# Tile 25's last rounding steps into slots 0 and 1 of block 1, tile 26 into slots 1 and 2, and batch 2's products of q one slot on

## The chip, the core and the metric

The kernel runs on one core of a Trainium2 chip. The metric is device time of one execution in microseconds (us): the median of five runs. The engines are TensorE (PE in the profile), VectorE (DVE), ScalarE (ACT), GpSimd (POOL) and SyncE (SP), which here only issues transfers. Each works through its own queue in order, and semaphores hold an instruction until what it needs is there.

## The reference

Two layers follow each other, all in float32:

```python
# q, k, v: (8 batches, 8 heads, 576, 64); g_norm: (64,)
kv  = einsum('bhsd,bhse->bhde', k, v)
out = einsum('bhsd,bhde->bhse', q, kv)
out = out / sqrt(mean(out * out, -1) + 1e-6) * g_norm
x   = out.transpose(0, 2, 1, 3).reshape(4608, 512)
h   = x @ w_in                       # w_in (512, 2048)
y   = maximum(0.01 * h, h) @ w_out   # w_out (2048, 512)
```

The weights come in as float64 and are rounded to float32 on the chip.

## The kernel before

**Blocks and units.** The 4608 rows of x are cut into 9 blocks of 512. A block goes through the two weight products in chunks of d_ff, 512 columns each (four chunks, numbered 0 to 3). Block 0 begins with plain products over chunks 0 to 2, in `first_block`; then comes block 1 over all four chunks, then chunk 3 of block 0, then blocks 2 to 8. One block and chunk is a *unit*. In a unit each of the two products is done in Strassen's manner with seven products, in the order 1, 2, 6, 5, 7, 3, 4.

**Slots.** The main loop gives each of the seven products h of a unit one *slot*: block 1 has slots 0 to 27, chunk 3 of block 0 has slots 28 to 34. A slot issues one product h (eight matmuls, 1.73 us from start to start), and from slot 9 on also one product o of an earlier unit, which stand in `o_queue` and lag by two slots. In slots 0 to 8 there is no product o beside the products h. The results of products h lie in four PSUM banks, `ha`, `hc`, `hb`, `hd`. Product 6 is added in the same bank on top of product 1, so it waits until ScalarE has copied product 1 out (L938); product 5 starts the second bank afresh, so it waits until VectorE has added product 2 into g (L698). In the same way product 7 waits for the copy of product 6 (L945), product 3 for the copy of product 5 (L940), and product 4 for VectorE's sum of product 7.

**Rounding the weights.** A weight tile (32 of them, `w_jobs`) is rounded by the generator `round_f64`, seven steps long: two ScalarE casts (L264 `add`, L262 `cut`), VectorE's clamp (L266), an empty step, the *sign* step on ScalarE (L271), VectorE's shift-and-or (L281) and, as the last step, VectorE's 16-bit add (L284). Tiles up to 25 are started in `first_block` by `round_w`, which does the first three steps and leaves the rest to `finish_w`; a table `plan` says at which half step which tile starts (a number) and where the open one is finished (`f`). From tile 26 on the main loop does the steps, 3, 3 and 1 in three slots, by the queue `rest`. Tiles 24 to 27 are the four tiles of w_out for chunk 3; chunk 3 is not used before slot 21.

**GpSimd and the writes.** GpSimd forms the sums of weight tiles and of g that the Strassen products take (`sides_w1`, `sides_w2`, `combine`, `sums_of`). Many are written to DRAM for the later blocks; SyncE issues these writes (L735) in a fixed order, behind the four writes of block 0's part sums `o` (`part<-o`), which VectorE (L1158) and ScalarE (L1156) copy out of PSUM at the end of `first_block`. The buffer `pairs` is used again as soon as its write has landed.

**Attention beside it.** `attention(b)` is a generator too: it turns q (L505), forms kv = k'v in PSUM, copies it to SBUF (`copy_kv`, L371), then for each block that the batch touches issues the products of q with kv (`outputs`, step for e = 0 and step for e = 1) with squares and scaled copies on ScalarE (L415, L421), sums of squares (L419), transposes and reductions (L430, L431), the root (L436), the reciprocal (L440), its spreading (L444), a transpose back and the multiply of x (L450, L452). The table `A_SLOTS` says how many steps of batch 2's attention are taken in which slot. Batch 2's first part writes 384 rows of block 2.

```python
            for t in range(7):
                slot = 7 * c + t
                go(h_steps, 1)
                ...
                    if rest:
                        go(steps, rest.popleft())
                    ...
                    go(a_steps, A_SLOTS.get(at, 0))
```

Of the kernel before, what the change touches and what calls it, by code (L numbers as in the profile page):

```python
# [24 lines left out]
def kernel(  # L25
# [121 lines left out]
    def load_some(n=1):  # L147

        while to_load and n > 0:
            b, p, what = to_load.popleft()  # L150
            load_pair(b, p, what)
            n -= 1
# [157 lines left out]
    def rounding(j, high_first=False):  # L310
        if w_in.dtype == I64:
            yield from round_f64(w_jobs[j][0], w_raws.pop(j), high_first)

    halfway = collections.deque()
# [15 lines left out]
    def finish_w():  # L330
        while halfway:
            for _ in halfway.popleft():
                pass
# [597 lines left out]
    def product_h(n, w_sides, x_sides, to):  # L931

        g11, g21, g22, g12 = g_of(n)

        def done(i, bank):

            if i == 1:
                first_turn(nc.scalar.copy(g11, bank))  # L938
            elif i == 5:
                first_turn(nc.scalar.copy(g22, bank))  # L940
            elif i == 2:
                add(nc.vector, g11, bank, g11, pinned=True)
                relu(g11)
            elif i == 6:
                first_turn(nc.scalar.copy(g21, bank))  # L945
            elif i == 3:
                add(nc.vector, g21, bank, g21, pinned=True)
                relu(g21)
            elif i == 7:
                add(nc.vector, g22, bank, g22, pinned=True)  # L950
                relu(g22)
            else:
                relu(g12, bank)

        yield from strassen((("ha", "hc"), ("hb", "hd"))[n % 2], lambda i, part, r: w_sides[i][:, part, r, :],
                            lambda i, part, r: x_sides[i][:, r, :], done)
        sums_of(n, to)
# [142 lines left out]
    def go(steps, n=None):  # L1100
        while n is None or n > 0:
            if next(steps, steps) is steps:
                return
            n = None if n is None else n - 1
# [20 lines left out]
    def first_block(between):  # L1125
# [27 lines left out]
        for t in range(4):  # L1153
# [9 lines left out]
    t, a, f, x = "tafx"  # L1163
# [2 lines left out]
            (5, 0): (13, f, a), (5, 1): (14, f), (6, 0): (15, f), (6, 1): (16, f),  # L1166
            (7, 0): (a, a, 17, f), (7, 1): (a, 18, f), (8, 0): (19, f, a, 20, f),
            (8, 1): (21, f, a), (9, 0): (a, a, a, a, a, a, 22, f), (9, 1): (x, 23),
            (10, 0): (f, 24), (11, 0): (f, 25), (12, 1): (f,)}
    loaded, x_sides = 12, None  # L1170

    def between(n, half):
        nonlocal loaded, x_sides
        for what in plan.get((n, half), ()):
# [7 lines left out]
            else:  # L1182
# [9 lines left out]
    first_block(between)  # L1192
    in_first = False
    first_done = True
    rounded, rest = 26, collections.deque()
    in_block_1 = True
    pin(nc.gpsimd.tensor_copy(pair(0, NW)[:1, :1], x_sides[4][:1, 0, :1]))
    h_sides, more = sides_w1(0)
# [4 lines left out]
    in_loop = True  # L1203

    LATE_ONE = {15: 2, 16: 2, 17: 1, 18: 1, 19: 2}
    A_SLOTS = {18: 1, 19: 2, 22: 1, 23: 1, 24: 2, 25: 1, 26: 1, 27: 2, 28: 1, 29: 1, 30: 1, 31: 1,
               34: 2}
    DIRECT = {25: ((1, (0, 1)), (3, (1,))), 27: ((2, (0, 1)),), 29: ((3, (0,)),)}
    READS = {26: 2, 28: 4, 30: RING}
    PARTS = {33: ("11", "12"), 35: ("22",), 37: ("21",)}  # L1210
# [13 lines left out]
    def second_of(n):  # L1224
        if n in seconds:
            os_, finish = seconds.pop(n)
            return Second(n, os_["11"], finish)
# [9 lines left out]
    for i, chunks in rounds:  # L1237
        one = in_block_1 = i < 2
        steady = not one
        if i == 1:  # L1240
            late, a_steps = a_steps, attention(2)
        elif i > 1:
            late, a_steps = a_steps, attention(i + 1, fine=True) if i + 1 < B else iter(())
        os = {}
        for c in chunks:
            now += 1
            nxt = units[now + 1] if now + 1 < len(units) else (NB, 0)
            g_sides = {}
            h_steps = product_h(now, h_sides, x_sides, g_sides) if one else \
                product_h_two(i, c, now, quarters, g_sides, second_of(now - 2))  # L1250
# [3 lines that stand above are left out]
                if not one:  # L1254

                    if t == 6:
                        go(h_steps, 1)
                    if slot in LATE_SLOTS:
                        go(late, 1)
                    for _ in range(FINE_SLOTS.get(slot, 0)):  # L1260
                        go(a_steps, 1)
                    if i + 1 < NB:
                        if slot == 20:
                            x_sides, new_quarters, sums, inner = sides_x(i + 1)
                        if slot in (20, 21, 22):
                            go(sums, 2 if slot == 20 else 1)
                        if slot == 24:
                            inner(0)
                        elif slot == 25:
                            inner(1)  # L1270
                    load_some()

                if now - 1 in seconds:
                    for half in range(2):
                        if t == (6 if half else 4):
                            inner_g(now - 1, half)
                    if t == 5 and now - 1 < 2 * NC + NC - K:
                        inner_w2(units[now - 1][1])
                if (7 * now + t == 7 * NC + 4):
                    while writes:  # L1280
                        pin(nc.sync.dma_start(*writes.pop()))
                if slot in HELD and i == NB - 1:
                    pass
                elif waited == LAG:
                    go_o()
                elif o_queue:
                    waited += 1
                write_later()
                at = 7 * now + t
                for key in PARTS.get(at, ()):  # L1290
                    if at == 33:
                        part_os = os
                    load_part(part_os, key)
                if at in READS:
                    read(READS[at])
                if one:
                    if not rest and rounded < len(w_jobs):
                        steps = rounding(rounded)
                        rest.extend((3, 3, 1))
                        rounded += 1  # L1300
                    if rest:
                        go(steps, rest.popleft())
                    if loaded < min(rounded + 2, len(w_jobs)):
                        load_w(loaded)
                        loaded += 1
                    for chunk, only in DIRECT.get(at, ()):
                        go(combine(chunk, 2, only=only))
                    if at == 18:
                        direct_0 = combine(0, 2, nc.vector)
                    if at in (18, 19, 22, 23):  # L1310
                        go(direct_0, 1)
                    if t == 3 and nxt[0] < 2 and nxt[1] != c:
                        h_sides, more_h = sides_w1(nxt[1])
                        if now == 0:
                            go(combine(0, 1))
                    if t == 5 and nxt[0] < 2 and nxt[1] != c:
                        more_h()
                    if t == 0 and units[now - 1][1] != c and now > 0:
                        for part in range(2):
                            go(combine(c, part))  # L1320
                    if at in (15, 16):
                        load_pair(2, at - 15)
                    go(late, LATE_ONE.get(at, 0))
                    go(a_steps, A_SLOTS.get(at, 0))
                    load_some(2 if at in (19, 20, 24, 25) else 1)
                    if at == 7 * NC - 4:
                        x_sides, _, sums, _ = sides_x(0)
                    elif at == 7 * N1 - 4:
                        x_sides, new_quarters, sums, inner = sides_x(2)
                    if at in (7 * NC - 4, 7 * NC - 3, 7 * N1 - 4, 7 * N1 - 3):  # L1330
                        go(sums, 2)
                    if at == 7 * N1 - 3:
                        inner(0)
                    elif at == 7 * N1 - 2:
                        inner(1)

            for _ in range(2 if i == NB - 1 and c == NC - 1 else 0):
                go(h_steps, 1)
                go_o()
            go(h_steps)  # L1340
            if c == NC - 1 and i != 1 and i + 1 < NB:
                inner(2)
                quarters = new_quarters
            by_two = NC + NC - K <= now < len(units) - 2
            if by_two:
                seconds[now] = (os, store(i))
            o_queue.append(product_o(now, g_sides, os, store(i), by_two))
# [32 lines left out]
```

## Time and profile before

| | |
|---|---|
| median of 5 runs | 919.46 us (919.02 to 920.09) |
| the profiled execution | 920.02 us, its span 918.3 us |
| PE busy | 907.2 us (99%) |
| DVE, ACT, POOL busy | 623.2, 347.6, 392.1 us (68%, 38%, 43%) |
| granted TensorE clock | 1.000 |

The span is the time from the first to the last instruction of the profiled execution; 1.7 us of its time lie around it. Times in the timeline count from the start of the span. A busy PE is no PE at its peak, as matmuls are pipelined and their ends are modelled; the start-to-start times are the safer reading. A wait for several semaphores is put down to the one that came last by the profile, and where the engine named had long been done it was another. Block 1 begins at about 113 us and ends at about 205 us, chunk 3 of block 0 ends at about 230 us.

### The profile page before, as it was taken

To read this page: it belongs to the slowest core of one execution; us is meant where nothing else is said; L and a number is where in the kernel's file an instruction comes from. 1 tells how busy PE (TensorE), PEld (TensorE's weight loads), DVE (VectorE), ACT (ScalarE), POOL (GpSimd) and SP (SyncE) were. 2 spreads that over 40 slices of the span, in tenths; PEclk is the share of its full clock that TensorE was granted. 3 is DMA by queue.
4 is the path that set the end of the run, shared out by engine and by line. 5 is a ranking of instruction groups with operands and counts; after the bars stand their busy time and mean duration, and the time that the engine had idled before them with its cause. 6 is when DMAs were issued, how large, how long until landed. Compare 5 with 4: busy or idle time off the path is not lost.

```text
span 918.3 us, 18136 instructions
## 1 busy us (share of the span) xinstructions
PE 907.2 (99%) x7024; PEld 783.9 (85%) x7024; DVE 623.2 (68%) x1127; ACT 347.6 (38%) x679; POOL 392.1 (43%) x467
## 2 busy tenths in 40 slices
PE   8999989999999999999999999999999999999998
PEld 4444478878998999899999999999999999999997
DVE  5765865767656876687756876678669755755565
ACT  5756454221335233433243334332443333223330
POOL 2000479959733473226421642264226522542222
PEclk9999999999999999999999999999999999999999
DMA  8998175896999678867886789757765676567632
GB/s 256 217 251 233 57 222 181 261 301 199 348 329 290 213 223 263 232 231 218 250 258 217 233 245 264 229 168 221 237 180 174 194 218 201 182 190 220 201 108 92
DMA packets 92405, 202.16 MB, mean 220 GB/s; under 512 B 10016, under 2 KB 44448, under 8 KB 92320
## 3 DMA queue, kind: packets, MB, share of 16 engines
q1 hardware_dynamic: 81344, 189.14, 68.6%
q10 hardware_dynamic: 10528, 10.69, 3.4%
q8 instruction: 56, 0.92, 0.4%
q0 software_dynamic: 448, 1.18, 0.3%
q14 instruction: 29, 0.24, 0.1%
HBM read 173.44 MB, written 27.53 MB: 219 GB/s over the span
## 4 chain that ended last, share of the span: by engine, by line
PE 77%; DMA 8%; POOL 7%; DVE 4%; issue 2%; ACT 1%; SPq 0%; POOLq 0%; ACTq 0%; DVEq 0%
PE o_c L126 17%; PE o_a L126 17%; PE h_ha L126 11%; PE h_hb L126 11%; PE h_hc L126 8%; PE h_hd L126 8%; POOL pairs L698 3%; PE o_ps L126 3%; POOL stage L698 2%; DMA stage<-in_moe_w_in_dram 2%; POOL gs L698 2%; DMA v_in<-in_v_dram 1%; DMA q_in<-in_q_dram 1%; DMA pairs<-in_moe_w_out_dram 1%; DMA pairs<-in_v_dram 1%
## 5 line engine op out<-in xcount | busy, mean ns | idle before, releaser
L698 POOL TENSOR_TENSOR gs<-g 128x512 f32<-128x512 f32 x66 | 84.1, 1274 | 249.0 <-ACT g L913 249.0
L913 ACT ACTIVATE g<-g 128x512 f32<-128x512 f32 x127 | 80.2, 631 | 148.6 <-DVE g L698 148.5
L1032 ACT COPY w_all<-h_ha 128x512 f32<-128x512 f32 x84 | 49.0, 583 | 169.7 <-PE h_ha L126 159.6
L126 PE MATMUL o_c<-pairs,gs 128*128 128x256 f32 x392 | 93.2, 381 | 0.0
L126 PE MATMUL o_a<-pairs,gs 128*128 128x256 f32 x392 | 93.0, 380 | 0.0
L698 DVE TENSOR_TENSOR o<-h_hb,o 128x128 f32<-128x128 f32 x104 | 29.9, 287 | 83.5 <-ACT pairs L1032 83.4
L126 PEld LDWEIGHTS o_c<-pairs,gs 128*128 128x128 f32 x392 | 71.3, 190 | 9.4 <-POOL pairs L698 1.2
L126 PEld LDWEIGHTS o_a<-pairs,gs 128*128 128x128 f32 x392 | 71.3, 190 | 8.1
L698 DVE TENSOR_TENSOR o<-o_a,o 128x512 f32<-128x512 f32 (+1 forms) x93 | 62.6, 673 | 22.0 <-PE o_a L126 21.7
L698 DVE TENSOR_TENSOR o<-o_c,o 128x512 f32<-128x512 f32 x80 | 54.7, 684 | 26.2 <-PE o_c L126 26.0
L126 PE MATMUL h_ha<-stage,w_all 128*128 128x128 f32 x448 | 59.6, 276 | 0.0
L126 PEld LDWEIGHTS h_ha<-stage,w_all 128*128 128x128 f32 x448 | 56.6, 192 | 3.0 <-issue 0.7
L698 DVE TENSOR_TENSOR g<-g,pairs 128x512 f32<-128x512 f32 x84 | 55.7, 689 | 1.9
L698 POOL TENSOR_TENSOR pairs<-g 128x128 f32<-128x128 f32 x52 | 23.8, 457 | 76.1 <-PE h_hb L126 47.4
L698 DVE TENSOR_TENSOR w_all<-h_hc,w_all 128x512 f32<-128x512 f32 x56 | 38.3, 685 | 15.7 <-PE h_hc L126 15.3
L698 DVE TENSOR_TENSOR o<-h_hd,o 128x128 f32<-128x128 f32 x78 | 22.2, 284 | 38.1 <-ACT pairs L1032 38.0
L126 PE MATMUL h_hb<-stage,w_all 128*128 128x128 f32 x336 | 46.7, 275 | 0.0
L698 POOL TENSOR_TENSOR gs<-g,gs 128x512 f32<-128x512 f32 x33 | 46.2, 1400 | 0.0
L698 POOL TENSOR_TENSOR gs<-gs,g 128x512 f32<-128x512 f32 x33 | 45.0, 1364 | 2.6
L1032 ACT COPY pairs<-h_hb 128x384 f32<-128x384 f32 x84 | 40.1, 477 | 13.2 <-PE h_hb L126 12.6
L126 PE MATMUL o_acc<-w,g 128*128 128x512 f32 x96 | 43.7, 598 | 0.6 <-DVE w L284 0.3
L126 PE MATMUL h_ha<-xT,w_all 128*128 128x128 f32 x224 | 43.3, 275 | 0.1
(240 smaller groups left out, 2245.1 us busy)
## 6 DMA issues: line engine op xcount, KB each, us to landing
w_all<-w SPq DMA_DIRECT2D x196, 448.0 KB, 4.1
pairs<-w SPq DMA_DIRECT2D x56, 512.0 KB, 4.4
out_dram<-o ACTq DMA_DIRECT2D x35, 256.0 KB, 4.9
v_in<-in_v_dram SPq DMA_DIRECT2D x27, 288.0 KB, 4.9
k_in<-in_k_dram SPq DMA_DIRECT2D x26, 288.0 KB, 4.3
q_in<-in_q_dram SPq DMA_DIRECT2D x52, 144.0 KB, 5.4
q_in<-in_q_dram SPq DMA_DIRECT2D x52, 140.0 KB, 5.4
w<-stage SPq DMA_DIRECT2D x12, 512.0 KB, 4.4
```

The lines of the kernel that those rows point to most:

```text
L126: pin(nc.tensor.matmul(*args, **kw))
L698: ins = eng.tensor_tensor(out_, a, b_, op=ALU.subtract if minus else ALU.add)
L913: first_turn(nc.scalar.activation(t, t if src is None else src, func=AF.Prelu, alpha=SLOPE))
L1032: nc.scalar.copy(q[:, at], bank)
```

## The change

Tile 25 is no longer finished at the end of `first_block`. Its queue is taken over by the main loop: in slot 0 its empty step, sign and shift-and-or, in slot 1 its last add. Tile 26 is started in slot 1 instead of slot 0 and takes its last four steps in slot 2, where it took three in slot 1 and one in slot 2. From slot 3 on (tile 27 and later) the slots are as they were. In `A_SLOTS`, steps 8 and 9 of batch 2 (the products of q with kv for e = 0 and e = 1) go from slots 25 and 26 to 26 and 27; its two steps of transposes and reductions go from slot 27 to slot 28; the root goes from slot 28 to slot 29, where the reciprocal and its spreading are as before. Later steps keep their slots. No instruction is added or taken away on a compute engine.

```diff
@@ plan of first_block
-            (10, 0): (f, 24), (11, 0): (f, 25), (12, 1): (f,)}
+            (10, 0): (f, 24), (11, 0): (f, 25)}
@@ ahead of the main loop
-    rounded, rest = 26, collections.deque()
+    rounded, rest = 26, collections.deque((3,))
+    steps = halfway[0]
@@ tables of the main loop
-    A_SLOTS = {18: 1, 19: 2, 22: 1, 23: 1, 24: 2, 25: 1, 26: 1, 27: 2, 28: 1, 29: 1, 30: 1, 31: 1,
-               34: 2}
+    A_SLOTS = {18: 1, 19: 2, 22: 1, 23: 1, 24: 2, 26: 1, 27: 1, 28: 2, 29: 2, 30: 1, 31: 1, 34: 2}
@@ in a slot of the main loop
                     if not rest and rounded < len(w_jobs):
+                        finish_w()
                         steps = rounding(rounded)
-                        rest.extend((3, 3, 1))
+                        rest.extend((3, 4) if rounded == 26 else (3, 3, 1))
                         rounded += 1
```

## The prediction

> **What bounds the kernel now.** I read the engine shares first, then TensorE's waits, then the timeline around each wait.
>
> ```profile
> PE 907.2 (99%) x7024; PEld 783.9 (85%) x7024; DVE 623.2 (68%) x1127; ACT 347.6 (38%) x679; POOL 392.1 (43%) x467
> ```
>
> TensorE is in use almost throughout, so the change, which takes no matmul away, can only win gaps on PE. The view of waits over 100 to 260 us, where everything moved lies, names them (total, times, longest, in us):
>
> ```profile
> PE h_c L126 <- DVE g L698: 1.6, 1, 1.6
> PE h_a L126 <- POOL stage L698: 1.1, 1, 1.1
> PE o_ps L126 <- DVE kv L371: 1.0, 1, 1.0
> PE h_b L126 <- ACT g L938: 0.3, 1, 0.3
> ```
>
> The timeline shows the first two, in slots 2 and 3 of block 1, and what stands in front of them:
>
> ```profile
> 114.19 1.49 DVE L266 TENSOR_SCALAR cut<-cut 128x512 f32<-128x512 f32 x1
> ...
> 115.71 0.64 ACT L271 ACTIVATE w<-cut 128x512 int32<-128x512 f32 x1 [3.00 <-DVE cut L266]
> 116.25 1.05 ACT L1156 COPY o<-o_acc 128x512 f32<-128x512 f32 x2
> ...
> 116.38 1.24 DVE L281 SCALAR_TENSOR_TENSOR w<-cut,w 128x512 uint32<-128x512 uint32 x1 [0.70 <-ACT w L271]
> ...
> 117.19 0.60 ACT L938 COPY g<-h_a 128x512 f32<-128x512 f32 x1
> 117.65 1.11 DVE L284 CUSTOM_DVE_ANT_0 w<-w,add 128x1024 uint16<-128x1024 uint16 x1
> ...
> 117.89 1.97 PE L126 MATMUL h_a<-xt,pairs 128*128 128x256 f32 x8 [1.12 <-POOL stage L698]
> ...
> 118.68 1.28 DVE L1158 COPY o<-o_acc 128x512 f32<-128x512 f32 x2
> ...
> 119.39 2.19 SPq L735 DMA_DIRECT2D part<-o  x4
> 119.88 0.97 DVE L266 TENSOR_SCALAR cut<-cut 128x512 f32<-128x512 f32 x1
> ...
> 120.77 0.68 DVE L698 TENSOR_TENSOR g<-h_c,g 128x512 f32<-128x512 f32 x1
> ...
> 121.50 1.99 PE L126 MATMUL h_c<-xt,pairs 128*128 128x256 f32 x8 [1.65 <-DVE g L698]
> ```
>
> Product 6 (117.89) is put down to POOL, but it waits for ScalarE's copy of product 1, which ends 0.10 us ahead of it (117.79). That copy stood behind tile 25's sign (L271), and this idled 3.00 us for the clamp. Product 5 (121.50) waits for `g<-h_c`, behind tile 25's L281 and L284, two copies and tile 26's clamp. The same queue holds `part<-o` on SP until 119.39, and behind that the writes that free `pairs`. The other wait and what the writes hold:
>
> ```profile
> 127.14 1.27 POOL L698 TENSOR_TENSOR pairs<-w_all 128x512 f32<-128x512 f32 x1 [5.17 <-DMA w<-pairs]
> 132.45 1.97 PE L126 MATMUL h_b<-xt,pairs 128*128 128x256 f32 x8 [0.32 <-ACT g L938]
> 195.67 0.46 DVE L371 COPY kv<-kv_ps 128x128 f32<-128x128 f32 x2
> 195.99 1.07 PE L126 MATMUL o_ps<-qT,kv 64*32 64x384 f32 x16 [0.98 <-DVE kv L371]
> ```
>
> **Slots 0 to 2: tile 25.** The built order of the changed kernel puts ScalarE's two copies (L1156) and L938 ahead of the sign, and on VectorE clamp, two copies, L281, `g<-h_c`, L284. Product 1 ends at 113.15 + 1.89 = 115.04, so L938 runs from 115.10 to 115.70 and product 6 starts at its regular time, 114.88 + 1.73 = 116.61: 1.28 earlier. On VectorE the clamp still ends at 115.68, the copies at 116.88, L281 (1.24, with POOL at work beside it) at about 118.05, `g<-h_c` at 118.65; product 5 starts at 118.70 where its regular time is 118.34. It comes 2.80 earlier, with a new wait of 0.36.
>
> A rule of the Trainium skill speaks against this place. L281 reads two SBUF inputs, and "SBUF — State Buffer", section "Who interferes with whom", says that such an instruction and a GpSimd one that reads SBUF exclude each other for their whole length. By it, L281 would stand until the POOL sum ending at 118.21 is done and then take its undisturbed time, an estimate of 118.9 for its end, which would take 0.85 from the sum and leave 1.9. The rows of L281 beside a busy POOL, 0.98 to 1.44 against 0.69 without it, hold whatever blocking there is, and I go by the nearest, tile 25's own 1.24.
>
> **Slots 1 to 9: what is late next.** Tile 26 now has six of its instructions in slots 1 and 2, with no products o to fill PE. ScalarE: relu (L913) at 118.70, L264 at 119.24, L262 119.81 to 120.48, L945 to 120.94. So product 7 starts at 121.00, 0.57 behind its regular time. VectorE's clamp of tile 26 starts at 120.50 and with its own row's 0.97 ends at 121.47; the sign runs to 122.11; L940, queued behind it, starts at 122.03. Product 3 is on time at 122.73. Tile 27's L264 then starts at about 122.5, where it started at 124.02. From there to the copy L938 of slot 9 before (131.74) only ScalarE and VectorE hand over to each other: relus, sign, L281, sum, tile 28's casts. This chain of 7.7 us keeps its order, product 6 of slot 9 still ends it, and so it comes as much earlier as the chain starts: **1.5 us** kept of the 2.80. With L281 at 0.69 (POOL idle) and the clamp at 0.43, the shortest rows, the chain starts near 121.4, a gain of 2.6; with L281 at 1.44 and the clamp at 1.49, the longest, near 123.2, a gain of 0.8.
>
> POOL must follow, since PE then needs its sums sooner. Its idle 5.17 us end when the writes of `pairs` land. They are issued behind `part<-o`, which VectorE's first copy releases at 116.25 instead of 119.3, 3.1 earlier. POOL then starts at about 124.0, and as it idles nowhere from there to 193.9 it stays some 3 us ahead. PE's nearest need, the g sum that ends at 139.61 for a product at 141.16, has 1.55 us in hand in any case. Tile 25's later end costs nothing: chunk 3 is first used in slot 21, and its two scratch buffers go to tile 27, whose first cast (122.5) comes 2 us behind tile 25's last add (L284, 118.6 to 120.3 with its longest row, 1.65).
>
> **Slots 25 to 29: q.** The products for e = 0 wait 0.98 for kv. From their regular time, 193.11 + 1.73 = 194.84, to the next product h at 196.99 they take 2.15; the e = 1 group, which does not wait, takes 0.90 (198.82 + 1.73 = 200.55 to 201.45). One slot later is 3.45 us of other work, kv is long there, and both cost 0.90: **1.25 us** gained (the wait of 0.98 and the restart after it). The slot's other steps go past this: product 5 of the o bank now comes at 196.57 instead of 198.82 and needs VectorE's sum ending at 195.74, still 0.8 in hand. This holds if VectorE moves up with PE: its chain here starts from a q turn at 176.8, which follows sums released by PE, so it does.
>
> The squares, sums and transposes come a slot later. VectorE's transposes and reductions (four of 0.57 and 0.55) then follow the o sum at 208.66 and end near 211.5; `g<-h_c` moves from 210.46 to 211.5, while the product that needs it comes at 215.36. Root (0.32), reciprocal (0.29) and spreading (0.92), queued behind relu L913, end near 214.4 on the old clock. The transpose back starts at 216.17: 1.8 in hand. No moved step issues a transfer, and SP's and POOL's queues keep their order.
>
> **The sum.** 1.5 + 1.25 = 2.75 us. On the profiled execution: span 918.3 to 915.55, time 920.02 to 917.3. That execution lies 0.56 above the median; from the median it is 919.46 - 2.75 = **916.7**. Behind 230 us PE is busy for 640 of 640 us, so what is gained by then is kept.
>
> **The rivals.** *The waits only move* (0.10): tile 26's hand-overs, squeezed in two slots, hold L940 until the old time, PE meets the old chain at slot 9, and only kv's wait goes. For it: that chain already ended last there (0.32 at 132.45). Against it: every row above would have to be longer by 1.5 us in sum. 919.46 - 1.25 = 918.2.
>
> *POOL does not follow* (0.10): the write of `pairs` lands when it did, because the DMA engines are full, or the next rewriting of `pairs` waits for its own write. Then PE meets POOL at the latest sum: the one ending at 219.97, for the product at 220.54, 0.57 in hand. The gain is capped at 0.6: 918.9. Against it: those writes landed in 3 to 4 us, and the writes ahead of them are released 3.1 earlier.
>
> *The root comes too late* (0.08), slower: two of the hand-overs squares, transposes, root, reciprocal each miss their place and lose a slot of 3.45. The spreading ends 6.9 - 1.8 = 5.1 late; from the transpose back to block 2's first products VectorE runs without a gap (219.02 to 229.46, then product at 230.66), so all of it goes to PE: 919.46 + 5.1 - 2.75 = 921.8. The kernel gets slower once the delay exceeds 1.8 + 2.75 = 4.55. Against it: the working above has 1.8 in hand.
>
> **How the numbers follow.** The forecast has 0.72. Its own range: 0.8 to 2.6 for the slots plus 0.98 (the wait alone) to 1.25 for kv, less up to 0.4 (one issue on SP) in the tight place ahead of block 2, where the sums of x end at 237.16 for a product at 237.34: 1.4 to 3.85, or 915.6 to 918.1. Taking in the two small gains and the spread of the runs: 915.2 to 919.1, which leaves out the slow rival and a little on either side. What this kernel's measurement can tell from no change is about 0.2%, 1.8 us, so faster means below 917.6: most of the forecast's own range, 0.69. Same: the two middling rivals and the forecast's upper end, 0.23. Slower: 0.08.
>
> **What would show it.** Right: no PE wait on kv; product 6 of slot 2 without a wait; small waits at products 5 and 7 (about 0.4 and 0.6); POOL's idle time ahead of slot 9 shrunk from 5.2 to about 2; slot 9's product near 130.9; block 2's first product near 227.9. Wrong: that last number within 1 us of 230.66, a PE wait on POOL `gs` or `stage` near 218 or 235, or on VectorE's `inv` and `xT` chain.

## The result, and the profile after

The changed kernel took 917.89 us (median of 24 runs, 916.58 to 921.02) where the kernel before took 919.07 (45 runs, 918.4 to 922.26): ratio 0.9987, 95% interval 0.9981 to 0.9992. It was run twice more beside the experiments, at 918.91 (0.9995, 0.9986 to 1.0003) and 916.87 (0.9977, 0.9968 to 0.9985). All 46 runs together have a median of 917.68, against 919.02 for the 95 runs of before beside them. So the gain is some 1.3 us or 0.15%, about half of the 2.75 forecast; and it moved by 2 us between sets, which the experiments explain in part.

The profiled execution took 917.99 us, its span 916.2. Of the 2.1 us that the span lost, 0.67 lie ahead of block 1 (its first product starts at 112.48 instead of 113.15). The same start moved between 111.76 and 113.41 over all profiles, with either version of `first_block` (111.98 to 113.15 with the old one), so no effect of the change can be read from it. From here on, *positions* are counted from that product. Behind block 2's first product the span has 687.6 to 687.7 us left in both kernels: what happens lies between.

| position of, us | before | after | moved |
|---|---|---|---|
| slot 9's product 6 | 19.30 | 16.85 | -2.45 |
| slot 28's first product | 91.85 | 88.26 | -3.59 |
| GpSimd's last sum before its idle time ends | 80.75 | 78.18 | -2.57 |
| GpSimd restarts behind `w<-stage` | 89.95 | 88.14 | -1.81 |
| the latest g sum ends | 106.82 | 106.34 | -0.48 |
| the product that needs it | 107.39 | 106.39 | -1.00 |
| block 2's first product | 117.51 | 116.04 | -1.47 |

The engine line and TensorE's waits over 100 to 260 us, after:

```profile
PE 906.7 (99%) x7024; PEld 783.9 (86%) x7024; DVE 622.2 (68%) x1127; ACT 347.2 (38%) x679; POOL 392.5 (43%) x467
```

```profile
PE o_c L126 <- POOL gs L698: 2.3, 1, 2.3
PE h_a L126 <- issue: 0.3, 1, 0.3
...
PE h_b L126 <- ACT g L938: 0.2, 1, 0.2
```

The waits of 1.6, 1.1 and 1.0 of before are gone, and a new one of 2.3 us, on GpSimd's g sum (tile `gs`), has come. The engines' timelines of the first slots, merged, show that the rounding part did more than was forecast:

```profile
115.63 1.81 SPq L735 DMA_DIRECT2D part<-o  x4
...
115.93 1.89 PE L126 MATMUL h_a<-xt,pairs 128*128 128x256 f32 x8
116.12 0.82 DVE L281 SCALAR_TENSOR_TENSOR w<-cut,w 128x512 uint32<-128x512 uint32 x1
...
117.66 1.94 PE L126 MATMUL h_c<-xt,pairs 128*128 128x256 f32 x8
...
119.91 1.97 PE L126 MATMUL h_a<-xT,pairs 128*128 128x256 f32 x8 [0.32 <-issue]
...
124.01 1.27 POOL L698 TENSOR_TENSOR pairs<-w_all 128x512 f32<-128x512 f32 x1 [2.64 <-DMA w<-pairs]
...
129.33 1.97 PE L126 MATMUL h_b<-xt,pairs 128*128 128x256 f32 x8 [0.23 <-ACT g L938]
```

Products 6 and 5 of block 1 come without a wait, product 7 with 0.32, and GpSimd's idle time ahead of slot 9 is 2.64 instead of 5.17. The same of the stretch from 195 to 221 us shows what then goes wrong. First the kernel before:

```profile
202.15 1.03 DVE L419 TENSOR_TENSOR sum<-sum,sq 128x384 f32<-128x384 f32 x2 [0.71 <-ACT sq L415]
...
203.10 0.73 POOL L698 TENSOR_TENSOR stage<-w_all 128x256 f32<-128x256 f32 x1 [9.20 <-DMA w<-stage]
...
216.75 1.27 POOL L698 TENSOR_TENSOR gs<-g 128x512 f32<-128x512 f32 x1
...
218.10 1.87 POOL L698 TENSOR_TENSOR gs<-gs,g 128x512 f32<-128x512 f32 x1
...
220.54 1.89 PE L126 MATMUL o_c<-pairs,gs 128*128 128x256 f32 x8
```

Then the changed kernel:

```profile
195.48 0.88 PE L126 MATMUL o_ps<-qT,kv 64*32 64x384 f32 x16
...
200.62 0.73 POOL L698 TENSOR_TENSOR stage<-w_all 128x256 f32<-128x256 f32 x1 [9.96 <-DMA w<-stage]
...
201.44 2.13 DVE L419 TENSOR_TENSOR sum<-sum,sq 128x384 f32<-128x384 f32 x2 [0.71 <-ACT sq L415]
...
202.11 1.05 POOL L698 TENSOR_TENSOR stage<-w_all 128x256 f32<-128x256 f32 x1
...
212.62 1.37 DVE L452 TENSOR_TENSOR xT<-xT,inv 128x768 f32<-128x768 f32 x1
...
213.12 1.17 POOL L698 TENSOR_TENSOR stage<-w_all 128x128 f32<-128x128 f32 x1
...
215.62 1.27 POOL L698 TENSOR_TENSOR gs<-g 128x512 f32<-128x512 f32 x1
...
216.96 1.86 POOL L698 TENSOR_TENSOR gs<-gs,g 128x512 f32<-128x512 f32 x1
...
218.87 1.99 PE L126 MATMUL o_c<-pairs,gs 128*128 128x256 f32 x8 [2.33 <-POOL gs L698]
```

The product of q (195.48) no longer waits for kv. But GpSimd idles 9.96 us until a write has landed, and then works through a fixed list of 22 sums before the first g sum. Before, that list took 13.65 us (203.10 to 216.75); here it takes 15.00 (200.62 to 215.62). The moved sums of squares L419, which ran ahead of GpSimd's restart before (202.15, two in 1.03 us), now fall on its stage sums. Both get longer: L419 2.13 us, the stage sums 1.05 and 1.03 instead of 0.73. A multiply L452 does the same to a small stage sum (1.17 instead of 0.46). 0.32 + 0.30 + 0.71 = 1.33 of the 1.35. L452 is not one of the moved steps. It came forward with TensorE, from position 103.63 to 100.14, while the list's start came only 1.81 forward: before, it began as the list ended (216.78 and 216.75); now it falls on the list's last part.

### The profile page after: what moved, and what is told of

The parts are those of the page before. It is cut to its first block, busy times and chain, and to the rows that moved or that the text cites. A ratio compares the mean times of both kernels' runs of the same rounds, so it can differ in the third digit from the quotient of the medians.

```text
span 916.2 us, 18138 instructions
## 1 busy us (share of the span) xinstructions
PE 906.7 (99%) x7024; PEld 783.9 (86%) x7024; DVE 622.2 (68%) x1127; ACT 347.2 (38%) x679; POOL 392.5 (43%) x467
## 4 chain that ended last, share of the span: by engine, by line
PE 79%; DMA 9%; DVE 5%; POOL 2%; ACT 2%; issue 2%; SPq 0%; DVEq 0%; ACTq 0%; POOLq 0%
PE o_c L126 18%; PE o_a L126 17%; PE h_ha L126 11%; PE h_hb L126 11%; PE h_hc L126 8%; PE h_hd L126 8%; PE o_ps L126 3%; DMA stage<-in_moe_w_out_dram 1%; POOL stage L698 1%; DMA pairs<-in_v_dram 1%; DMA pairs<-in_moe_w_out_dram 1%; DMA q_in<-in_q_dram 1%; DVE g L698 1%; DMA pairs<-in_moe_w_in_dram 1%; PE h_a L126 1%
## 5 line engine op out<-in xcount | busy, mean ns | idle before, releaser
L126 PE MATMUL h_hd<-xT,w_all 128*128 128x128 f32 x224 | 43.3, 275 | 0.0
```

Source lines behind the costliest of these rows:

```text
L126: pin(nc.tensor.matmul(*args, **kw))
```

## The experiments

Two theories were put up first. A: GpSimd's latest g sum limits what TensorE can gain, and the q part drives TensorE into it. B: the 2.3 us wait on gs is an accident of the profiled execution. All were timed in five rounds beside the kernel before on the same chip.

| kernel | us | ratio to before (95%) | list of sums, us | wait on gs, us | g sum ends | block 2's first product |
|---|---|---|---|---|---|---|
| before | 919.0 | 1 | 13.65 | none | 106.82 | 117.51 |
| after, first profile | 917.89 | 0.9987 (0.9981-0.9992) | 15.00 | 2.33 | 106.34 | 116.04 |
| after, second | 918.91 | 0.9995 (0.9986-1.0003) | 14.93 | 2.60 | 106.15 | 117.52 |
| after, third | 916.87 | 0.9977 (0.9968-0.9985) | 14.86 | 0.3 | 105.35 | 115.36 |
| rounding part alone | 916.85 | 0.9979 (0.9970-0.9987) | 13.63 | none | 104.17 | 114.86 |
| q part alone | 920.33 | 1.0014 (1.0005-1.0023) | 14.88 | 1.7 | 107.80 | 117.50 |
| after, one sum later | 916.24 | 0.9970 (0.9959-0.9982) | 12.36 | none | 103.87 | 115.09 |
| the same again | 916.10 | 0.9964 (0.9952-0.9976) | 12.36 | none | 103.32 | 114.54 |
| rounding part, one sum later | 916.35 | 0.9969 (0.9956-0.9981) | 11.85 | none | 102.86 | 115.17 |
| q part, one sum later | 918.38 | 0.9989 (0.9980-0.9998) | 12.48 | none | 105.78 | 116.62 |
| after, other homes | 917.98 | 0.9985 (0.9976-0.9994) | - | none | 102.20 | 114.68 |
| after, g sum twice | 918.58 | 0.9995 (0.9987-1.0004) | 14.86 | 2.02 | 107.18 | 116.87 |
| after, g sum four times | 923.71 | 1.0049 (1.0036-1.0062) | 14.86 | 5.39 | 111.08 | 122.24 |
| after, short L419 | 916.89 | 0.9977 (0.9965-0.9988) | 13.65 | none | 103.94 | 114.86 |

The last four columns are of the profiled execution of each, the last two as positions. The wait of 0.3 of the third profile is the gap between the regular start, 215.16 + 1.73 = 216.89, and the product at 217.16, 0.05 behind the sum's end; the view of waits does not list it.

**The changed kernel again, and each part alone.** The rounding part alone keeps the old `A_SLOTS`; the q part alone keeps the old `plan` and `rest`.

> The changed kernel once more, beside the others on one chip. Theory A (GpSimd's g sum caps the gain): TensorE has its slots 0 to 9 and the q products 3.6 us earlier, and gives 2.0 to 2.6 us of it back in one wait on GpSimd's gs near 218 us; 1.0 to 1.5 us faster than before. Theory B (the wait on gs was an accident of one execution): no wait on gs over 1 us in this profile.

> The rounding part alone (tiles 25 and 26), the attention slots as before. Both theories: slot 9 comes 2.4 us earlier, the wait of about 1 us on kv stays. Theory A: VectorE's sums of squares then run ahead of GpSimd's stage sums as before, GpSimd is faster by 0.6 us, TensorE comes 1.1 us later than in the changed kernel, so the wait on gs shrinks to 0.4 to 1.0 us: 1.3 to 1.9 us faster than before, at least as fast as the whole change. Theory B: no wait on gs, 2.4 us faster than before.

> The attention part alone (products of q one slot on), tiles 25 and 26 as before. Both theories: no wait on kv, 1.1 us won there. Theory A: only 0.57 us are in hand at the gs sum, and VectorE's sums of squares now fall beside GpSimd's stage sums and slow them by 0.6 us, so a wait on gs of 0.6 to 1.2 us takes it back: 0 to 0.5 us faster than before. Theory B: 1.1 us faster.

The second set has the wait on gs that A expected (2.60), but only 0.1 us of gain (918.91 against 919.03), where A had 1.0 to 1.5. Six of its eleven runs show a lower TensorE clock, which is taken up below, where the g sum is lengthened.

The gain is all in the rounding part, and more than all: 2.2 us, with no wait on gs, where A had expected a small one. A's numbers are a miss here, and B's forecast (no such wait, 2.4 us faster) lies nearer. The reason is instructive, and it is not B's: with the rounding part alone GpSimd does follow. Its restart moves by 2.64 (position 89.95 to 87.31), TensorE's slot 28 by 2.58. From the timeline of that kernel:

```profile
199.82 1.03 DVE L419 TENSOR_TENSOR sum<-sum,sq 128x384 f32<-128x384 f32 x2 [0.71 <-ACT sq L415]
...
200.72 0.72 POOL L698 TENSOR_TENSOR stage<-w_all 128x256 f32<-128x256 f32 x1 [9.14 <-DMA w<-stage]
```

L419 still ends as GpSimd begins, and the list takes 13.63. The q part alone is slower than the kernel before, on which neither theory had counted. In the profile TensorE gains 1.45 up to slot 28 (91.85 to 90.40) and gives all of it back in the wait on gs (block 2's first product at 117.50 and 117.51), as the list takes 14.88. In the median of its runs it is 1.3 us slower, not equal; what comes on top is seen below, where the g sum is lengthened.

**One sum of the list put off.** The part of a weight sum that slot 25 issued goes to slot 28, behind the g sums.

```diff
-    DIRECT = {25: ((1, (0, 1)), (3, (1,))), 27: ((2, (0, 1)),), 29: ((3, (0,)),)}
+    DIRECT = {25: ((1, (0, 1)),), 27: ((2, (0, 1)),), 28: ((3, (1,)),), 29: ((3, (0,)),)}
-    ... (3, 2): (4, 5)}
+    ... (3, 2): (4, 3)}
```

> The changed kernel with one combination of chunk 3's weights (four GpSimd sums of 0.46 us, 1.85 us in all) moved from slot 25 to slot 28, behind the four gs sums, and its staging place with it. Theory A: the gs sum comes 1.8 us earlier, the wait on gs falls from 2.3 to about 0.5 us, and the kernel is 1.5 to 1.9 us faster than the changed one, if the sums of x for block 2 still come in time (0.2 us in hand). Theory B: as fast as the changed kernel.

> The changed kernel with the one stage sum put off to slot 28, once more, as the changed kernel itself moved by 2 us between sets of runs (917.89, 918.91, 916.87). Theory A (its time moves because TensorE's wait on gs is there in some executions and not in others; without that wait the time is steady): 915.9 to 916.8 where the kernel before takes 918.9 to 919.2, no wait on gs, no run with a low clock. Theory B (sets of runs differ by 1 to 2 us whatever the kernel, and the first set of this one was a lucky one): 917 or more, or a range of runs over 2 us wide.

The list is 2.6 us shorter, the wait on gs is gone, and the kernel is 2.7 us faster than the changed kernel on the same chip (918.91 to 916.24), more than A's 1.5 to 1.9. That is against the slowest of the changed kernel's three sets. Against all its 46 runs (917.68) it is 1.4 us, and against the fastest set 0.6. It is 2.8 us faster than the kernel before, and a second set on another chip gave 3.2. The runs of the first set lie within 0.43 us, of the second within 1.17, where the changed kernel's lie within 2.5 to 4.4. In steadiness and time both sets fall to A.

**The two parts with that sum put off.**

> The rounding part alone, with the one stage sum put off from slot 25 to slot 28 as in the fastest kernel so far (916.24). Theory A (the q part is worth its 1.1 us wherever GpSimd's g sum is not in the way, and putting off the sum does nothing where there is no wait on gs): the time is that of the rounding part alone, 916.85 within 0.4, 0.3 to 1.1 us above the fastest kernel; the wait of about 0.9 us on kv is there. Theory B (the q part costs something of its own, and it is the moved stage sum that gains): 916.2 or less, no slower than the fastest kernel.

> The q part alone, with the one stage sum put off from slot 25 to slot 28. Theory A (the q part gains 1.1 us on TensorE, and loses it to the g sum): the wait of 1.7 us on gs is gone or under 0.6, and the kernel is 0.6 to 1.3 us faster than the kernel before: 917.8 to 918.5 where that takes 919.05. Theory B (the q part costs something of its own): as slow as the q part alone, 919.3 to 920.5.

The q part alone now gains 0.8 us where it had lost 1.3, as A said: the loss was the g sum. But on top of the rounding part it is worth nothing that these runs can tell (916.35 without it, 916.24 and 916.10 with it), where A had 0.3 to 1.1. Putting off the sum also took the rounding part from 916.85 to 916.35, on another chip, though its profile had no wait on gs to lose; what gained there is not shown. In that kernel without the q part the wait on kv is 0.2, not 0.9, since TensorE waited 1.0 for a VectorE sum `o` just ahead (at about 190 us). This wait of 0.6 to 1.0 is there in eight of the eleven profiles with the rounding part, so in the third of the changed kernel:

```profile
190.63 1.97 PE L126 MATMUL o_a<-pairs,gs 128*128 128x256 f32 x8 [1.01 <-DVE o L698]
```

Just ahead of that sum VectorE works on two stage sums of its own, which begin when another write `w<-stage` has landed (186.4 to 187.4 us). What the q part avoids and what comes ahead of it take each other's place.

**GpSimd's wait for the write taken away.** Six stage sums get other buffers, so that GpSimd need not wait at 191 us.

```diff
-    ... (1, 2): (2, 4), (2, 2): (0, 2), (3, 2): (4, 5)}
+    ... (1, 2): (4, 0), (2, 2): (2, 0), (3, 2): (4, 1)}
```

> The changed kernel with other homes for six of the stage sums of chunk 3, so that GpSimd need not wait until the write w<-stage has landed (it idles 9.96 us for it, to 200.62). Theory A (GpSimd's late g sum is what caps the gain, and it is late because GpSimd restarts with the landing of that write): GpSimd goes on within 3 us of 191, the first g sum of the unit starts at least 1.7 us earlier than 215.62, TensorE's wait of 2.3 us on gs is gone; something smaller can come up at block 2's first products, up to 1.2 us, as the sums of x then wait for another write. 1.1 to 2.3 us faster than the changed kernel: 916.2 to 917.4 where that takes 918.6. Theory B (the g sum is late because VectorE slows GpSimd in the stretch behind 200 us, whenever it begins): the start moves, the g sums stay within 0.5 us of where they were, and at least 1.5 us of the wait stays: 918 to 919.

The wait on gs is gone, as A said, with the sum ending 4.1 us earlier. But the time, 917.98, is within the sets of the changed kernel, where A had 1.1 to 2.3 less. The waits of that kernel name two others:

```profile
PE h_ha L126 <- POOL stage L698: 1.1, 1, 1.1
PE o_a L126 <- POOL stage L698: 1.0, 1, 1.0
```

The second is the wait for VectorE's sum `o` of the other kernels, put down to GpSimd here: its product starts 0.15 us behind the end of that sum (190.98 to 191.13), just as in the third profile of after (190.48 to 190.63). The first is new. The buffers now wait for their writes elsewhere: GpSimd idles 5.3 us at 210 and 4.9 us at 230, and the sums of x that block 2 needs come late. Block 2's first product comes 1.4 us earlier than in the first profile of after, and 1.4 more is left behind it (689.06 us where the other has 687.68). GpSimd and its writes are a second chain beside TensorE's, with little slack in more than one place.

**The g sum lengthened.** The first g sum of that unit is done twice, then four times (the diff shows the second).

```diff
         add(nc.gpsimd, s1, g21, g22)
+        if n == 3:
+            for _ in range(3):
+                add(nc.gpsimd, s1, g21, g22)
```

> The changed kernel with the first of the four g sums of block 1's last unit done twice on GpSimd, some 0.7 to 1.3 us more in front of the sum that TensorE waits for. Theory A (that sum is the path, and TensorE's clock drops behind a gap of more than about 2 us): the wait on gs grows from 2.3 or 2.6 to 3.0 to 3.9 us, a low clock follows it in nearly all runs, and the time is 1.5 to 3 us above the changed kernel's: 920.1 to 921.6 where that takes 918.6. Theory B (the wait on gs is an accident of the profiled execution, and what follows has room for it): the time stays within 0.5 us of the changed kernel's.

> The changed kernel with the first g sum of block 1's last unit done four times on GpSimd: some 3.8 us more in front of the sum that TensorE waits for. Theory A (that sum is the path; a gap of 2 to 2.6 us lowers TensorE's clock in some runs, a longer one in all): the wait is 5.0 to 6.5 us, every run shows the low clock, and the time is 4.5 to 6 us above that of the changed kernel on the same chip. Theory B (the low clock has another cause than the gap): 3.3 to 4 us above, with the low clock in no more runs than the changed kernel has.

Twice is inconclusive in time: 0.7 us above the changed kernel's first set, 0.3 below its second, and 1.7 above the third, which ran on the same chip. A's wait of 3.0 to 3.9 and its low clock in nearly all runs did not come: the wait was 2.02, as TensorE itself came 1.14 later (slot 28 at 89.40, not 88.26), and 3 of 11 runs show the low clock. Its profile has the sum's end 0.84 later than in the first profile of after, and block 2's first product 0.83 later. Four times settles it. From its timeline, and its windows of 2 us (columns: length, busy us of PE, PEld, DVE, ACT, POOL, then TensorE's granted clock, DMA share, GB/s):

```profile
215.04 6.21 POOL L698 TENSOR_TENSOR gs<-g 128x512 f32<-128x512 f32 x4
...
222.99 3.45 PE L126 MATMUL o_c<-pairs,gs 128*128 128x256 f32 x8 [5.39 <-POOL gs L698]
```

```profile
220.00:222.00 2.00, 0.00 (x0) 0.00 (x0) 1.97 (x3) 0.00 (x0) 1.92 (x2) 1.00 1.04 348
222.00:224.00 2.00, 1.01 (x2) 0.84 (x3) 0.41 (x1) 0.63 (x1) 2.00 (x2) 0.64 0.95 237
224.00:226.00 2.00, 2.00 (x6) 1.64 (x5) 0.00 (x0) 0.00 (x0) 2.00 (x3) 0.51 1.00 334
```

The wait is 5.39, and behind it the clock falls to half for some 3 us: the product takes 3.45 instead of 1.89. The kernel takes 6.84 us more than the changed kernel on that chip, above A's 4.5 to 6, since that set of the changed kernel had hardly a wait on gs. Against the profile of that set, block 2 starts 6.88 later by position: 5.74 are there when this product starts, 1.14 come in the low clock behind it. The second profile of after shows the same behind its 2.60:

```profile
218.00:220.00 2.00, 1.79 (x5) 1.50 (x6) 1.97 (x2) 0.00 (x0) 2.00 (x3) 0.68 1.05 347
220.00:222.00 2.00, 2.00 (x6) 1.59 (x5) 1.40 (x3) 0.63 (x1) 2.00 (x2) 0.50 0.96 256
```

The first profile, with a wait of 2.33, kept 1.00 all along. From that product to block 2 the second took 11.32, the first 9.65. Over single runs of the changed kernel, the 11 (of 46) with a mean granted clock of 0.998 have a median of 919.42, the 31 at 1.000 have 917.39 (four lie at 0.999). How long each of these runs waited on gs is not on record, so the 2.0 between them can hold more than the clock. The q part alone had 5 such runs of 12 (921.45, the others 919.22, so without them it is close to the kernel before, 919.03), the sum done twice 3 of 11, four times 5 of 5. The short L419 below had 1 of 10, the other six sets without a wait on gs in their profile none in 50.

**Less of L419.** The two sums of squares take 64 of their 384 columns; that part of the norm is left out.

> The changed kernel, with VectorE's two sums of squares of batch 2's first part (L419, at 201.4 us) cut to 64 of their 384 columns; that part of the norm is left out. Theory A (GpSimd loses 1.3 us because the moved VectorE sums fall on its stage sums): the two L419 take under 0.6 us in sum, not 2.1, the stage sums beside them go back to 0.73, the list from GpSimd's restart to the first g sum takes 13.6 to 14.2 us instead of 15.0, TensorE's wait on gs goes from 2.3 to 1.0 to 1.7, and the median is 0.5 to 1.5 us below that of the changed kernel on the same chip. Theory B (GpSimd's slower list comes from transfers or from the xT multiplies, not from these sums): the list keeps 14.8 to 15.0 us, the wait its 2.0 to 2.6, and the time stays within 0.3 us.

The part of L419 is shown: the two sums take 0.50 us, the stage sums beside them keep their undisturbed time, the list takes 13.65 again, and the wait on gs is gone. L452 was not changed, and its 0.71 went too, because here it began behind the end of the list (214.12 and 213.30). That L452 lengthens the list is read from the overlap in the timelines, not from an experiment of its own. The time is a miss for A: 916.89 beside 916.87 for the changed kernel on that chip, since that set of the changed kernel hardly waited for gs either.

> The changed kernel once more, beside the two others on the same chip. Both theories: 917.4 to 919.0 where the kernel before takes 919.1, a wait of 2.0 to 2.6 us on gs. Theory A: the runs split by TensorE's clock, those at the full clock near 917.5, those with a dip 1.3 to 2 us above.

This third set was faster than either theory had it, and shows one reason why the kernel's time moves. GpSimd restarts at 199.64, and L419 (201.94) falls behind the large stage sums, on small ones (0.77 and 0.65, not 0.46); the list is only 0.14 shorter. The second g sum escapes (1.27 us, not 1.86), which gives most of what follows: it ends at position 105.35 instead of 106.34. TensorE had waited 1.0 for `o` at 190 us, and so has only 0.3 left to wait. Both engines move by 0.3 to 1.7 us from one execution to the next (GpSimd's restart at 88.14, 88.02 and 87.88, slot 28 at 88.26, 87.79 and 89.48), and the wait on gs is what is left between them, 2.3, 2.6 or 0.3, with a low clock behind it at times. It is not the only reason: of the 1.4 us between the spans of the first and third profile, 0.72 lie ahead of block 1, where nothing differs between them.

## Why the prediction was half right

**The sign and the range were right, the size was not.** 917.89 lies within 915.2 to 919.1, 1.2 above the point; the outcome held likeliest, faster by over 0.2%, did not come, as 0.13% is what the text called no change (0.23). The rows named as right are there: no wait on kv, product 6 of slot 2 free, a small wait at product 7. The second sign named as wrong is there as well: a PE wait on POOL `gs` near 218. That the time fell in the range is in part luck: TensorE gained 0.8 more than forecast up to slot 28 (3.59 for 2.75), and then lost 2.5 to a wait that the sum did not have.

**Slots 0 to 9: forecast 1.5, measured 2.45.** The chain was read rightly, and the term was sized with rows that were too long. By position, the chain's start (tile 27's L264) came 2.07 earlier, not 1.5, and the chain itself took 7.32 instead of 7.72, as tile 27's L281 took 1.01 and not 1.44. Tile 25's L281 took 0.82 where 1.24 was assumed, tile 26's clamp 0.86 for 0.97, and tile 27's L264 started at 121.28 (121.95 on the clock of before) for 122.5. The wait of 0.36 at product 5 did not appear; product 7 started 0.52 behind its regular time, for 0.57. Over the eleven profiles with the rounding part slot 9 comes 1.6 to 2.7 earlier; in three of them TensorE waits 1.2 for VectorE's sum `g` in slot 6. GpSimd stood elsewhere too: L281 (116.12 to 116.94) met the end of a stage sum that ended at 116.39, not the one that the forecast put beside it, and the next stage sum took 1.19 instead of 0.73. The rule from "SBUF — State Buffer", section "Who interferes with whom", would block L281 until 116.39 and then let it take its 0.69 alone, an estimated end of 117.08, and put the next sum, with its 0.73, to an estimated 117.81; the rows have 116.94 and 117.54. What was off in the forecast by the rule, 118.9 (118.2 on the clock of after), was which sum L281 meets.

**Slots 25 to 29: forecast 1.25 on TensorE, measured 1.14 in this profile**, as slot 28's product moved by 3.59. The wait on kv and its removal were read rightly. But the condition named for it was not checked far enough: "its chain here starts from a q turn at 176.8, which follows sums released by PE, so it does". VectorE's timeline of the kernel before has, behind that turn, an idle time for a write:

```profile
189.09 0.29 DVE L698 TENSOR_TENSOR stage<-w_all 128x128 f32<-128x128 f32 x1 [5.13 <-DMA w<-stage]
```

So VectorE came only 1.45 forward here where TensorE came 2.45. The sum `o` behind it, which had 1.30 in hand before (191.81 for a product at 193.11), was just in time (189.98 for 190.13). Of the nine profiles with both parts it was late in seven, and there slot 28's product moved by 1.9 to 2.5 only, where the rounding part without the q part moved it by 2.58 and 1.76.

**"POOL must follow ... it stays some 3 us ahead" is the step that failed.** It followed the idle time to 193.9 us and stopped there. Of the 3.1, there were 2.46 at GpSimd's restart ahead of slot 9 (position 13.99 to 11.53), and it was still 2.57 ahead at its last sum (position 80.75 to 78.18, the very 78.17 of the rounding part alone). But behind that stood 9.2 us of idle time for the write of `stage`, for which the step had no price. The write was issued 2.33 earlier and took 4.65 to the restart instead of 4.13 (3.84 to 4.65 over the profiles): 1.81 ahead. Then the list lost 1.35: 0.48 ahead. TensorE meanwhile came 3.59, with 0.57 in hand: 3.59 - 0.57 - 0.48 = 2.5 of new stall; the wait is 2.33 and the product 2.48 behind its regular start. The q step looked at who issues and at the order of GpSimd's queue, and both were unchanged; it did not look at what runs beside VectorE's sums: the two L419 that it moved, and L452, which comes forward with TensorE.

**The rivals.** "POOL does not follow" named the place, the sum of 219.97 with 0.57 in hand, and had a chance of only 0.10. Its cause, full DMA engines or a late write of `pairs`, was not the one, and its cap of 0.6 was too tight, since GpSimd came forward by 0.48 and smaller gaps behind closed by 0.47: 1.0 + 0.47 = 1.47 at block 2. "The waits only move" and "The root comes too late" did not happen: slot 9 kept its gain, and no profile has a wait on the root's chain.

What stays open: what makes the clock fall in one execution with a wait of about 2.5 us and not in the next, and how far the landing times of the writes differ by chip rather than by run.

## What to carry to other kernels

Ask of every engine that hands something to the bottleneck not only whether it starts earlier, but whether it is still earlier at its last hand-over; a wait for a transfer on the way sets its own time. Two gains on the bottleneck do not add up when the second one moves only the bottleneck: of the two parts here, one alone gave 2.2 us and the other alone lost 1.3. And when an instruction is moved, look at what runs beside it in its new place on the engines that it slows.

## What the runs showed of the hardware

- TensorE's clock fell to about half for some 3 us behind a gap of 2.60 us and of 5.39 us, not behind 2.33, 2.02 and 1.65 in one profile each. It cost 1.1 to 1.7 us in the profiles; runs of the changed kernel that show it lie 2.0 above the others in the median. "TensorE: Matmul & The Clock Gate" of the Trainium skill (Part 1) puts the slow clock behind an idle window of about 3.4 us in a free-running count, and asks for no idle gap over that. The 5.39 would bring it by that rule, and did; 2.60 would not, and did, so a shorter gap is not safe here.
- Where VectorE sums or multiplies of two inputs and GpSimd sums overlapped, mostly both got longer: two L419 from 1.03 to 2.13 us, a stage sum of 128x256 from 0.73 to 1.05, one of 128x128 from 0.46 to 1.17. Not always both: in the kernel before, L452 took 2.06 (0.96 at the shortest) beside a g sum that kept its 1.27. For an engine whose list is fixed, 0.3 to 0.7 us at each such meeting is a price to count when an instruction is moved.
